# Splitting q and k of fused attention in fewer, wider pieces: block-diagonal last rows, one low part on VectorE, and another order of the period

## The chip, the cores and the metric

The kernel runs on one core of a Trainium2 chip. Times are microseconds of device time for one execution. The core has TensorE (PE in the rows; its weight loads are PEld), VectorE (DVE), ScalarE (ACT), GpSimd (POOL), SyncE (SP, which starts most of the DMA transfers here), a memory on the chip that all of them read (SBUF), and a smaller one for the results of TensorE (PSUM).

## The reference

Attention with a block-causal mask over 8 batches of 8 heads, then a mixture of experts (16 experts in 4 groups, one expert for each token).

```python
B, H, S, D = q.shape                       # 8, 8, 576, 64
scores = scale * np.matmul(q, k.transpose(0, 1, 3, 2))
mask = block_i >= block_j                  # blocks of 64 positions
scores = np.where(mask, scores, -1000000000.0)
scores = scores - np.max(scores, axis=-1, keepdims=True)
attn = np.exp(scores)
attn = attn / (np.sum(attn, axis=-1, keepdims=True) + 1e-09)
attn_out = np.matmul(attn, v)
x = attn_out.transpose(0, 2, 1, 3).reshape(B * S, H * D)   # 4608 x 512
...
g_idx = np.argmax(x @ w_group, axis=1)     # then an expert of the group
h = np.maximum(xg[mask_e] @ w1[g, e], 0.0)
out[tok_idx] = combined[:, None] * (h @ w2[g, e])
```

## The kernel before, in words

The attention works on items. An item is two heads of one batch (the two heads lie in the two halves of the 128 partitions), so there are 32 items, four to a batch. The kernel writes out one period for each item. A period is a list of tokens, `ORDER`, and a token is a letter, a number and a lag: `S3@0` in period x is step S3 of item x, `k1@-1` is step k1 of item x+1. The list is the program order on every engine, and each engine works through its own instructions in that order. A letter `d` behind the lag puts a copying step on VectorE, other copying steps are ScalarE's.

The steps of an item, in the order of its data:

- K: q and k are transposed on TensorE (16 transposes of 64 rows), their first 512 rows. k0 and k1 copy the result to the SBUF tile `nf` (k0 for k, k1 for q times 0.125).
- The last 64 rows of q and k are transposed in step V of an earlier item (`values`), behind its products, into the same PSUM tile `o`. j0 and j1 copy them to `nf`.
- h0 and h1 (`high`) round k and q to the shorter type fp32r, l0 and l1 (`low`) store what rounding left, `nf - high`. The results are in `qk`. For q the last 64 columns are stored block-diagonally, the first head on partitions 0 to 63 and the second on 64 to 127, with zeros elsewhere, so h1 and l1 take three instructions each: 512 columns, and 64x64 twice.
- S3, S2, S1, S8: scores, each the sum of three products in this order: high q with high k, high q with low k (needs l0), low q with high k (needs l1). S2 also does the pair 0.
- D: the row maximum on VectorE. E: the exponential on ScalarE (E6 and E7 belong to S3, E5, E4, E1 and E0 to S2, E3 and E2 to S1, E8 to S8).
- T: transposes of the result on TensorE, t: its copy to SBUF on ScalarE. V: the products with v, v: the copy of the result to `xT`.
- L, n, Y, M, R, X, G, Z: the router and the normalized output of a batch whose four items are done; in each period some of them run. Z are scatters that GpSimd starts.

PSUM gives four buffers of one width in turn (`wide`): every K, S, T, V, L, Y, X and G4 takes the next one, and waits until the tile four places back has been read by all who read it.

The experts follow the attention, on TensorE nearly without a gap. `Attention.start` does the first item ahead of the periods.

Of the kernel before, what the change touches and what calls it, by code (L numbers as in the profile page):

```python
# [48 lines left out]


ORDER, ON_DVE = parse("""
D8@1 Z2@8 E3@1 E2@1 X1@6 K@-1 S3@0 E8@1 k1@-1a S2@0 L0@3 k0@-1a D3@0 E7@0 E6@0 G4@6 D0@0 D2@0 E5@0 G3@6 E0@0
E1@0 R0@3 V@2 T4@1 E4@0 G2@5 G0@4 j0@-1d Z4@9 n0@3a j1@-1d t4@1a v@2d h0@-1 X2@4 T2@1 h1@-1 Y0@3 X0@5 l1@-1
M0@3 T1@1 t2@1a L1@2 T3@0 l0@-1 t0@1a Y1@3 t1@1a t3@0a G1@4 n1@2d S1@0 D1@0 Z0@7 Z1@8 Z3@11 M1@3 S8@0
""")

LAST = [("G", 0), ("G", 1), ("G", 2), ("G", 4), ("G", 3)] + [("X", j) for j in range(3)] + [("Z", j) for j in range(NT)]
# [2 lines left out]
class Attention:  # L60
    def __init__(self, tc, ctx, inner, q, k, v, consts):
        self.tc, self.nc = tc, tc.nc
        self.q, self.k, self.v = q, k, v
        self.c = consts
        self.xpool = ctx.enter_context(tc.tile_pool(name="xp", bufs=2))
        self.pt = ctx.enter_context(tc.tile_pool(name="pt", bufs=2))
        self.small = ctx.enter_context(tc.tile_pool(name="small", bufs=3))
        self.vfix = vfix = ctx.enter_context(tc.tile_pool(name="vfix", bufs=1))
        self.ctx = ctx
        self.psx = ExitStack()  # L70
        self.ps2 = self.psx.enter_context(tc.tile_pool(name="ps2", bufs=4, space=PSUM))
# [100 lines left out]
    def regions(self, i, n):
        al, lo, hi = slice(0, P), slice(0, 64), slice(64, P)
        if n == 0:
            return [(al, slice(0, S), 0)]
        return [(al, slice(0, 512), S), (lo, slice(512, S), S), (hi, slice(512, S), S + BLK)]
# [101 lines left out]
    def values(self, i, N):  # L278
# [1015 lines left out]
```

## Time and profile before

| | |
|---|---|
| median of 3 runs | 861.62 us (860.65 to 863.86) |
| the profiled execution | 854.16 us, of which the span of instructions is 852.4 us |
| PE busy | 796.1 us, 93% of the span |
| VectorE, ScalarE, GpSimd busy | 59%, 58%, 38% |
| mean granted TensorE clock | 0.983 |

The shares are averages over the attention (up to about 371 us), a passage to the experts, and the experts (from about 399 us); the engines are loaded quite differently in them. Rows below give a start and a length in us from the start of the span. Where a group of instructions is printed in one line, "x4" is their count and the shape is that of the first.

### The profile page before, as it was taken

The numbers are of one execution on the slowest core, as the hardware profiler recorded it, in microseconds if no ns is written. First come the engines' busy times: TensorE is split into PE (matmuls) and PEld (weight loads), VectorE is DVE, ScalarE is ACT, GpSimd is POOL, SyncE is SP. The second block draws the span as 40 slices with busy tenths as digits, with TensorE's granted clock in tenths as the row PEclk, the third lists the DMA queues.
The fourth block names the chain that finished last, engine by engine and source line by source line (L and its number), as shares of the span: only waits on it lengthen the run. The fifth ranks groups of instructions, "written<-read, shape, count | busy, mean of one in ns | idle before, by whom it ended". The sixth has DMA issues, their size and how long they took to land.

```text
span 852.4 us, 20362 instructions
## 1 busy us (share of the span) xinstructions
PE 796.1 (93%) x7617; PEld 648.4 (76%) x7617; DVE 500.6 (59%) x1136; ACT 496.0 (58%) x1210; POOL 324.9 (38%) x601
## 2 busy tenths in 40 slices
PE   7789899999999999888999999999999999999996
PEld 4666666666666666566888888888888889898885
DVE  4445868687777676678543454464453755656552
ACT  5877888888888888654332443433443544545441
POOL 5764546474747475643321221221221221132101
PEclk9999999999999999899999999999999999999998
DMA  6554554545454535263443746645555666575471
GB/s 126 137 143 121 152 135 93 135 93 135 93 135 86 142 82 132 62 210 107 155 141 100 237 160 197 202 130 184 196 165 152 189 210 196 180 224 181 150 238 39
DMA packets 182260, 126.69 MB, mean 149 GB/s; under 512 B 124902, under 2 KB 156214, under 8 KB 182160
## 3 DMA queue, kind: packets, MB, share of 16 engines
q1 hardware_dynamic: 173072, 100.73, 42.5%
q0 software_dynamic: 9088, 24.64, 8.5%
q8 instruction: 61, 1.00, 0.5%
q14 instruction: 39, 0.32, 0.1%
HBM read 100.88 MB, written 24.59 MB: 147 GB/s over the span
## 4 chain that ended last, share of the span: by engine, by line
PE 52%; DVE 1%; POOLq 0%; issue 0%; ACT 0%; ACTq 0%
PE y L999 19%; PE h L954 18%; PE y L1004 5%; PE h L949 4%; PE ye L999 2%; PE xp L922 2%; PE he L954 2%; POOLq L1290 0%; DVE gsc L709 0%; DVE gdd L707 0%; DVE goh L711 0%; DVE pre L739 0%; PE spill L609 0%; ACT ys L1021 0%; DVE sel L721 0%
## 5 line engine op out<-in xcount | busy, mean ns | idle before, releaser
L239 ACT ACTIVATE pb<-s,nm 128x512 f32<-128x512 f32 (+4 forms) x288 | 155.6, 556 | 57.0 <-DVE nm L227 51.5
L227 DVE TENSOR_REDUCE nm<-s 128x2 f32<-128x1024 f32 (+4 forms) x160 | 123.3, 807 | 67.2 <-PE s L222 60.9
L954 PE MATMUL h<-xt,wh 128*128 128x264 f32 (+6 forms) x704 | 155.3, 312 | 0.0
L906 DVE TENSOR_TENSOR wl<-raw,wh 128x512 fp32r<-128x512 f32 x192 | 123.3, 685 | 11.2 <-ACT wh L905 10.7
L218 PE MATMUL s<-qk 64*128 64x512 f32 (+3 forms) x768 | 96.0, 361 | 32.6 <-POOL qk L189 18.1
L954 PEld LDWEIGHTS h<-xt,wh 128*128 128x128 f32 x704 | 119.3, 188 | 9.1
L1028 POOL DMA_INDIRECT out_dram<-ys,ids x40 | 41.2, 1030 | 184.7 <-DVE ys L1024 171.2
L905 ACT CAST wh<-raw 128x512 fp32r<-128x512 f32 x192 | 108.8, 620 | 2.2 <-DMA raw<-in_moe_w_dram 1.9
L954 PE MATMUL h<-xt,wl 128*128 128x264 f32 (+6 forms) x352 | 109.3, 311 | 0.0
L999 PE MATMUL y<-wh,hring 128*128 128x512 f32 x306 | 107.2, 401 | 0.0
L272 ACT COPY pt<-tp 128x1024 f32<-128x1024 f32 (+4 forms) x160 | 100.9, 714 | 7.8 <-PE tp L148 6.4
L189 POOL TENSOR_TENSOR qk<-nf,qk 128x512 fp32r<-128x512 f32 (+1 forms) x124 | 101.6, 830 | 7.4
L301 PE MATMUL o<-pt,vb 128*64 128x320 f32 (+4 forms) x896 | 97.1, 370 | 0.0
L967 ACT ACTIVATE hring<-h 128x288 fp32r<-128x288 f32 (+7 forms) x62 | 28.9, 467 | 113.5 <-PE h L954 55.3
L218 PEld LDWEIGHTS s<-qk 64*128 64x128 f32 x768 | 61.5, 196 | 43.7 <-POOL qk L189 23.9
L182 POOL CAST qk<-nf 128x512 fp32r<-128x512 f32 (+1 forms) x127 | 53.7, 448 | 103.9 <-DVE nf L270 100.2
L971 DVE SCALAR_TENSOR_TENSOR hring<-h,hring 128x32 fp32r<-128x32 f32 (+7 forms) x112 | 35.7, 357 | 97.2 <-ACT hring L967 94.0
L301 PEld LDWEIGHTS o<-pt,vb 128*64 128x64 f32 x896 | 61.1, 141 | 36.2 <-issue 6.4
L869 POOL DMA_INDIRECT xg<-xd,ids x40 | 41.2, 1030 | 102.1 <-DMA ids<-tab 51.7
L148 PE MATMUL tp<-ident,pb 64*128 64x64 f32 x1600 | 63.5, 225 | 6.1 <-ACT pb L239 3.9
L954 PEld LDWEIGHTS h<-xt,wl 128*128 128x128 f32 x352 | 66.2, 188 | 1.2
L999 PEld LDWEIGHTS y<-wh,hring 128*128 128x128 f32 x306 | 57.6, 188 | 11.8
(237 smaller groups left out, 1342.8 us busy)
## 6 DMA issues: line engine op xcount, KB each, us to landing
raw<-in_moe_w_dram SPq DMA_DIRECT2D x96, 512.0 KB
natk<-in_k_dram SPq DMA_DIRECT2D x32, 256.0 KB
natq<-in_q_dram SPq DMA_DIRECT2D x32, 256.0 KB
vb<-in_v_dram SPq DMA_DIRECT2D x64, 128.0 KB
wh<-in_moe_w_dram SPq DMA_DIRECT2D x16, 512.0 KB
xd<-xns SPq DMA_DIRECT2D x14, 512.0 KB
tab<-fill POOLq DMA_DIRECT2D x10, 512.0 KB, 3.1
rawe<-in_moe_w_dram SPq DMA_DIRECT2D x8, 512.0 KB
```

Of the source, the lines that this page charges most:

```text
L148: self.nc.tensor.transpose(out=out[:, z], in_=src[r], identity=self.c["ident"][r, r])
L182: eng.tensor_copy(r["qk"][p, 0, a.start + o:a.stop + o], r["nf"][p, n, a])
L189: eng.tensor_tensor(out=r["qk"][p, 1, o], in0=r["nf"][p, n, a], in1=r["qk"][p, 0, o].bitcast(F32), op=ALU.subtract)
L218: nc.tensor.matmul(st[:, z, :], lhsT=t[p, hq, S + P * u:S + P * u + P], rhs=t[p, hk, 0:w], start=x == 0, stop=False)
L227: self.nc.vector.tensor_reduce(out=o, in_=r["s", u], op=ALU.max, axis=ax, negate=True)
L239: nc.scalar.activation(reg, src, AF.Exp, bias=r["nm"][:, t:t + 1], accum_out=self.sms[b][:, pr, z, u:u + 1])
L272: return self.nc.scalar.copy(dst, src)
L301: nc.tensor.matmul(o[64 * a:64 * a + 64, hf, c0:c0 + BLK * (b1 - t)], lhsT=r["v"][:, a, j, :], rhs=pt[:, PTJ * j + t:PTJ * j + b1, a, :], ...
L905: nc.scalar.copy(h[:, sl], s["raw", u][:, sl])
L906: nc.vector.tensor_tensor(out=l[:, sl], in0=s["raw", u][:, sl], in1=h[:, sl].bitcast(F32), op=ALU.subtract)
L954: nc.tensor.matmul(o, lhsT=ww[:, dc, f], rhs=rr[:, dc, t], start=dc == 0 and x == 0, stop=dc == 3 and x == 2)
L999: nc.tensor.matmul(y[c][0:n], lhsT=hh, rhs=w, start=k == 0 and x == 0, stop=k == 7 and x == 2)
```

## The change

Four edits:

1. The last rows of the second head of q are loaded three columns away, beside columns that were set to zero once (`natk` is now a pair of fixed tiles). The transposes then give the block-diagonal form directly (three of them instead of two). `nf` has room for it, j1 copies 128 columns, and h1 and l1 are one instruction each of 640 columns.
2. l0, the low part of k, is on VectorE, one instruction of 576 columns.
3. The order of the period is another one. In it k1 is on VectorE and j0, j1 and v are on ScalarE (before: k1 on ScalarE, j0, j1 and v on VectorE).
4. With the order, lags change: S8 is done a period later, E2 and E3 at the end of their own period, some router steps earlier or later by a period.

```diff
 ORDER, ON_DVE = parse("""
-D8@1 Z2@8 E3@1 E2@1 X1@6 K@-1 S3@0 E8@1 k1@-1a S2@0 L0@3 k0@-1a D3@0 E7@0 E6@0 G4@6 D0@0 D2@0 E5@0 G3@6 E0@0
...
+K@-1 Z3@10 S8@1 k1@-1d S3@0 D8@1 D3@0 k0@-1a S2@0 Z1@9 E8@1 Z4@8 G4@6 E6@0 Z0@8 Z2@9 D0@0 L1@3 E7@0 D2@0
...
-        self.nf = [pfix.tile([P, 2, S], F32, name=f"nf{i}") for i in range(2)]
+        self.nf = [pfix.tile([P, 2 * S + BLK], F32, name=f"nf{i}") for i in range(2)]
+        self.natk = [pfix.tile([P, 12, D], F32, name=f"natk{i}") for i in range(2)]
...
-        for t in self.qk:
-            nc.gpsimd.memset(t.bitcast(F32)[:, :, S + 512:], 0.0)
+        for t in self.natk:
+            nc.gpsimd.memset(t[64:128, 9:11, :], 0.0)
...
-            nc.sync.dma_start(out["k"][64 * z:64 * z + 64, 8:10, :],
+            nc.sync.dma_start(out["k"][64 * z:64 * z + 64, 8:10 + 2 * z:1 + 2 * z, :],
                               src[nm][b, h0:h0 + 2, 512:576, :].rearrange("a p d -> p a d"))
...
+    def flip_last(self, i, ps):
+
+        x = self.lds[i]["k"]
+        for z, n in ((0, 0), (1, 0), (1, 1)):
+            r = slice(64 * z, 64 * z + 64)
+            o = 384 * z + 64 * n
+            self.nc.tensor.transpose(out=ps[:, z, o:o + 64], in_=x[r, 8 + 2 * n:10 + 2 * n, :].rearrange("p a d -> p (a d)"),
+                                     identity=self.c["ident"][r, r])
...
     def full_last(self, i, n):
         r = self.rs[i]
-        self.evac(("j", n), r["nf"][:, n, 512:S], self.last(r["jps"])[:, n], 0.125 if n else None)
...
+        w = 64 + 64 * n
+        self.evac(("j", n), r["nf"][:, S * n + 512:S * n + 512 + w], r["jps"][:, n, 384 * n:384 * n + w], 0.125 if n else None)
+
+    def side(self, tok):
+        return self.nc.vector if tok in self.on_dve else self.nc.gpsimd
 
     def high(self, i, n, eng=None):
         r = self.rs[i]
-        eng = eng or self.nc.gpsimd
-        for p, a, o in self.regions(i, n):
-            eng.tensor_copy(r["qk"][p, 0, a.start + o:a.stop + o], r["nf"][p, n, a])
+        o = slice(S, 2 * S + BLK) if n else slice(0, S)
+        (eng or self.side(("h", n))).tensor_copy(r["qk"][:, 0, o], r["nf"][:, o])
 
     def low(self, i, n, eng=None):
         r = self.rs[i]
-        eng = eng or self.nc.gpsimd
-        for p, a, o in self.regions(i, n):
-            o = slice(a.start + o, a.stop + o)
-            eng.tensor_tensor(out=r["qk"][p, 1, o], in0=r["nf"][p, n, a], in1=r["qk"][p, 0, o].bitcast(F32),
-                              op=ALU.subtract)
+        o = slice(S, 2 * S + BLK) if n else slice(0, S)
+        (eng or self.side(("l", n))).tensor_tensor(out=r["qk"][:, 1, o], in0=r["nf"][:, o], in1=r["qk"][:, 0, o].bitcast(F32),
+                                              op=ALU.subtract)
```

How the order moves the instructions, at three places. First GpSimd, the split of one item. Before (CAST is `high`, TENSOR_TENSOR is `low`; k has 576 columns, q 512 and two squares):

```order
L182 CAST qk_113<-nf_115 128x576
L182 CAST qk_113<-nf_115 128x512
L182 CAST qk_113<-nf_115 64x64 x2
L189 TENSOR_TENSOR qk_113<-nf_115,qk_113 128x512
L189 TENSOR_TENSOR qk_113<-nf_115,qk_113 64x64 x2
L189 TENSOR_TENSOR qk_113<-nf_115,qk_113 128x576
```

and with the change, in a period in which a batch's scale factors (`ry`) are copied too:

```order
L187 CAST qk_113<-nf_115 128x576
L648 COPY ry_4585<-rx_4579 128x2x5x2 x2
L187 CAST qk_113<-nf_115 128x640
L192 TENSOR_TENSOR qk_113<-nf_115,qk_113 128x640
L187 CAST qk_114<-nf_116 128x576
```

Eight instructions of an item became three, and the one for the low part of k is gone from here.

Second VectorE, at the turn from one period to the next, in a period with the router's choice of experts (`esc` to `eoh`). Before:

```order
L707 TENSOR_TENSOR edd_3426<-el_3423,emx_3425 128x20
L709 SCALAR_TENSOR_TENSOR esc_3427<-edd_3426,desc 128x20
L710 TENSOR_REDUCE em_3428<-esc_3427 128x5
L711 TENSOR_TENSOR eoh_3429<-esc_3427,em_3428 128x20
L227 TENSOR_REDUCE nm_3270<-s_1_3437 128x2
L227 TENSOR_REDUCE nm_3270<-s_8_3449 128x1
L227 TENSOR_REDUCE nm_3487<-s_3_3488 128x2
```

and with the change:

```order
L710 TENSOR_TENSOR edd_2487<-el_2484,emx_2486 128x20
L712 SCALAR_TENSOR_TENSOR esc_2488<-edd_2487,desc 128x20
L713 TENSOR_REDUCE em_2489<-esc_2488 128x5
L714 TENSOR_TENSOR eoh_2490<-esc_2488,em_2489 128x20
L192 TENSOR_TENSOR qk_113<-nf_115,qk_113 128x576
L230 TENSOR_REDUCE nm_2333<-s_1_2499 128x2
L273 TENSOR_SCALAR nf_116<-tp_2519 128x512
L230 TENSOR_REDUCE nm_2333<-s_8_2536 128x1
L230 TENSOR_REDUCE nm_2546<-s_3_2547 128x2
```

The low part of k (l0, line 192) and the copy of q (k1, line 273) now stand between the router's steps and the row maxima D1, D8 and D3.

Third ScalarE, from the exponentials of S2 (E4 and its neighbours) to the copies of the transposes. Before:

```order
L239 ACTIVATE pb_117,sm_3485<-s_2_3925,nm_3913 128x384
L272 COPY lt<-lg_0_3942 128x2x288
L272 COPY pt_3844<-tp_4_3987 128x2x5x64
L272 COPY pt_3844<-tp_2_4005 128x2x3x128
L272 COPY pt_3844<-tp_2_4005 128x256
L272 COPY pt_3844<-tp_1_4051 128x2x2x128
L272 COPY pt_4061<-tp_3_4062 128x2x4x128
```

and with the change:

```order
L242 ACTIVATE pb_119,sm_1691<-s_2_1706,nm_1693 128x384
L275 COPY nf_116<-o_1741 128x64
L276 ACTIVATE nf_116<-o_1741 128x128
L275 COPY xT_1324<-o_1741 128x576
L275 COPY pt_1577<-tp_1_1781 128x2x2x128
L275 COPY pt_1577<-tp_4_1790 128x2x5x64
L275 COPY pt_1825<-tp_3_1826 128x2x4x128
L275 COPY pt_1577<-tp_2_1845 128x2x3x128
L275 COPY pt_1577<-tp_2_1845 128x256
```

j0, j1 and v (lines 275 and 276, from `o`) stand behind the last exponential of S2, and the copies t come in another order, with t2 and t0 last.

## Rows read from the trace of the kernel before

**Rows 1.** The time by stage: busy time of each engine in stretches of the span (start:end, length, then us busy and number of instructions for PE, weight loads, VectorE, ScalarE, GpSimd; then the granted TensorE clock, the DMA share and GB/s).

```profile
29.05:101.34 72.29, 61.44 (x869) 45.72 (x865) 38.22 (x78) 55.31 (x154) 42.58 (x98) 0.93 0.52 138
101.34:342.50 241.16, 220.67 (x3495) 166.94 (x3491) 178.46 (x419) 205.34 (x567) 140.03 (x253) 1.00 0.48 114
...
399.00:852.40 453.40, 446.32 (x2490) 386.83 (x2489) 229.92 (x501) 185.35 (x363) 97.46 (x161) 0.99 0.54 170
```

**Rows 2.** Waits, the window from 101.34 to 342.5 us (engine and line, what released it: us in total, times, longest).

```profile
PE s L218 <- POOL mark L782: 10.1, 11, 1.2
PE s L218 <- POOL qk L189: 7.3, 11, 0.7
```

**Rows 3.** TensorE in order of time: starts of the products with v (line 301), one for each period, and two of the waits of line 218 (start us, length us, engine, line, operation, count, idle time before and its releaser).

```profile
29.05 2.93 PE L301 MATMUL o<-pt,vb 128*64 128x256 f32 x28
...
39.21 1.22 PE L218 MATMUL s<-qk 64*128 64x512 f32 x4 [2.66 <-POOL qk L189]
...
42.42 4.37 PE L301 MATMUL o<-pt,vb 128*64 128x256 f32 x28
...
101.34 2.93 PE L301 MATMUL o<-pt,vb 128*64 128x256 f32 x28
...
342.50 2.92 PE L301 MATMUL o<-pt,vb 128*64 128x256 f32 x28
...
354.13 1.22 PE L218 MATMUL s<-qk 64*128 64x512 f32 x4 [4.12 <-POOL mark L782]
...
357.33 2.95 PE L301 MATMUL o<-pt,vb 128*64 128x256 f32 x16
...
364.61 2.92 PE L301 MATMUL o<-pt,vb 128*64 128x256 f32 x28
```

**Rows 4.** One period in order of time, all engines, 199.89 to 214.66 us.

```profile
199.89 2.92 PE L301 MATMUL o<-pt,vb 128*64 128x256 f32 x28
...
202.75 0.27 PE L148 MATMUL o<-ident,natk 64*128 64x64 f32 x2
...
203.51 1.69 POOL L182 CAST qk<-nf 128x576 fp32r<-128x576 f32 x4 [5.64 <-DVE nf L270]
...
205.28 3.43 POOL L189 TENSOR_TENSOR qk<-nf,qk 128x512 fp32r<-128x512 f32 x4
...
208.77 0.73 PE L218 MATMUL s<-qk 64*128 64x512 f32 x4 [0.70 <-POOL qk L189]
...
209.66 2.42 DVE L227 TENSOR_REDUCE nm<-s 128x2 f32<-128x1024 f32 x3 [1.73 <-PE s L222]
...
210.53 0.72 PE L670 MATMUL lg<-xT,wcat 64*32 64x288 f32 x16
...
210.92 0.69 ACT L239 ACTIVATE pb<-s,nm 128x512 f32<-128x512 f32 x1 [1.16 <-DVE nm L227]
...
211.18 2.93 PE L301 MATMUL o<-pt,vb 128*64 128x256 f32 x28
...
214.06 0.67 ACT L272 COPY lt<-lg 128x576 f32<-128x576 f32 x1
...
214.66 3.08 ACT L272 COPY pt<-tp 128x640 f32<-128x640 f32 x5
```

**Rows 5.** Busy time of the engines in the four periods of one batch, 145.03 to 188.76 us (columns as in rows 1).

```profile
145.03:188.76 43.73, 40.02 (x636) 30.32 (x632) 32.51 (x77) 37.28 (x104) 25.84 (x48) 1.00 0.46 111
```

**Rows 6.** Groups of instructions by line and shape, up to 390 us (line, engine, operation, names, shapes, count; us busy, mean ns of one; idle time before).

```profile
L189 POOL TENSOR_TENSOR qk<-nf,qk 128x576 fp32r<-128x576 f32 x31 | 43.5, 1404 | 2.4
L189 POOL TENSOR_TENSOR qk<-nf,qk 128x512 fp32r<-128x512 f32 x31 | 39.8, 1284 | 2.6
...
L189 POOL TENSOR_TENSOR qk<-nf,qk 64x64 fp32r<-64x64 f32 x62 | 19.6, 315 | 2.3
...
L182 POOL CAST qk<-nf 128x576 fp32r<-128x576 f32 x31 | 20.6, 665 | 94.6 <-DVE nf L270 94.5
...
L227 DVE TENSOR_REDUCE nm<-s 128x1 f32<-128x576 f32 x32 | 24.1, 754 | 6.3 <-PE s L208 6.3
...
L270 DVE TENSOR_SCALAR nf<-tp 128x512 f32<-128x512 f32 x1 | 0.7, 692 | 5.8 <-ACT nf L272 5.8
...
L189 DVE TENSOR_TENSOR qk<-nf,qk 128x512 fp32r<-128x512 f32 x1 | 0.7, 717 | 0.0
...
L272 ACT COPY nf<-o-3_167 128x64 f32<-128x64 f32 x1 | 0.2, 217 | 0.0
```

**Rows 7.** VectorE and GpSimd at the same time: a row of each at about 8 us, and three rows of both at about 139 us (start us, length us).

```profile
7.78 0.90 POOL L182 CAST qk<-nf 128x512 fp32r<-128x512 f32 x1 [5.68 <-DVE nf L270]
...
8.24 1.04 DVE L189 TENSOR_TENSOR qk<-nf,qk 128x576 fp32r<-128x576 f32 x1
...
136.02 0.18 DVE L707 TENSOR_TENSOR gdd<-lgs,gmx 128x20 f32<-128x20 f32 x1
...
139.79 3.42 POOL L189 TENSOR_TENSOR qk<-nf,qk 128x512 fp32r<-128x512 f32 x4
...
139.88 1.22 DVE L707 TENSOR_TENSOR edd<-el,emx 128x20 f32<-128x20 f32 x1
```

**Rows 8.** The period that begins at 342.50 us on GpSimd, and a stretch of 2 us with the granted clock (PEclk, 0.50) (columns as in rows 1).

```profile
350.35 0.23 POOL L182 CAST qk<-nf 64x64 fp32r<-64x64 f32 x1 [1.67 <-DMA tab<-pay,pi]
...
42.00:44.00 2.00, 2.00 (x16) 1.54 (x18) 1.29 (x2) 1.42 (x5) 1.13 (x8) 0.50 0.26 68
```

More of the change, by code (lines that the diff above doesn't have):

```diff
@@ L51 @@
 ORDER, ON_DVE = parse("""
-D8@1 Z2@8 E3@1 E2@1 X1@6 K@-1 S3@0 E8@1 k1@-1a S2@0 L0@3 k0@-1a D3@0 E7@0 E6@0 G4@6 D0@0 D2@0 E5@0 G3@6 E0@0
-E1@0 R0@3 V@2 T4@1 E4@0 G2@5 G0@4 j0@-1d Z4@9 n0@3a j1@-1d t4@1a v@2d h0@-1 X2@4 T2@1 h1@-1 Y0@3 X0@5 l1@-1
-M0@3 T1@1 t2@1a L1@2 T3@0 l0@-1 t0@1a Y1@3 t1@1a t3@0a G1@4 n1@2d S1@0 D1@0 Z0@7 Z1@8 Z3@11 M1@3 S8@0
+K@-1 Z3@10 S8@1 k1@-1d S3@0 D8@1 D3@0 k0@-1a S2@0 Z1@9 E8@1 Z4@8 G4@6 E6@0 Z0@8 Z2@9 D0@0 L1@3 E7@0 D2@0
+Y1@4 X2@5 G3@6 E0@0 V@2 n1@3d E5@0 E1@0 E4@0 M1@4 j0@-1a h0@-1a G2@5 j1@-1a Y0@3 T1@1 T4@1 R0@2 X1@5 h1@-1a
+l1@-1a v@2a X0@6 L0@2 t1@1a T3@0 t4@1a n0@2a t3@0a M0@3 T2@1 t2@1a t0@1a G0@4 G1@4 l0@-1d S1@0 D1@0 E2@0
+E3@0
 """)
@@ L124, in load @@
         out, src = {}, dict(k=self.k, q=self.q)
-        for nm, n in (("k", 10), ("q", 8)):
-            out[nm] = self.nat.tile([P, n, D], F32, tag="nat" + nm, name=f"nat{nm}{i}")
+        out["k"], out["q"] = self.natk[i % 2], self.nat.tile([P, 8, D], F32, tag="natq", name=f"natq{i}")
+        for nm in "kq":
             nc.sync.dma_start(out[nm][:, 0:8, :].rearrange("p (c a) d -> p c a d", a=2),
@@ L158, in prep @@
                 self.flip(o[:, :, c, :], ld[nm][:, 2 * c:2 * c + 2, :].rearrange("p a d -> p (a d)"))
-    def last(self, ps):
-        return ps.rearrange("p z (h c) -> p (z h) c", c=64)[:, 0:15:14, :]
+    def flip_last(self, i, ps):
[5 more added lines that the diff above has]
+                                     identity=self.c["ident"][r, r])
@@ L163, in full @@
     def full(self, i, n):
         r = self.rs[i]
-        self.evac(("k", n), r["nf"][:, n, 0:512].rearrange("p (z c) -> p z c", z=2), r["kps"][:, :, 256 * n:256 * n + 256],
-                  0.125 if n else None)
+        self.evac(("k", n), r["nf"][:, S * n:S * n + 512].rearrange("p (z c) -> p z c", z=2),
+                  r["kps"][:, :, 256 * n:256 * n + 256], 0.125 if n else None)
     def full_last(self, i, n):
         r = self.rs[i]
-        self.evac(("j", n), r["nf"][:, n, 512:S], self.last(r["jps"])[:, n], 0.125 if n else None)
@@ L172, in regions @@
[L172 to L176, printed above, removed]
+        w = 64 + 64 * n
+        self.evac(("j", n), r["nf"][:, S * n + 512:S * n + 512 + w], r["jps"][:, n, 384 * n:384 * n + w], 0.125 if n else None)
+    def side(self, tok):
+        return self.nc.vector if tok in self.on_dve else self.nc.gpsimd
@@ L285, in values @@
         if i + 3 < N:
-            self.flip(self.last(o), self.lds[i + 3]["k"][:, 8:10, :].rearrange("p a d -> p (a d)"))
+            self.flip_last(i + 3, o)
     def products(self, i, o):
```

## The prediction

> **What bounds the kernel now.** I read the time by stage first. From 399 us on, TensorE is busy for 446.3 of 453.4 us [rows 1], and the change touches nothing there: this part moves earlier or later as a whole. In the attention TensorE is not full. Over the 22 periods from 101.34 to 342.5 us it is busy 220.7 of 241.2 us at full clock, and in the six from 29.05 to 101.34 us 61.4 of 72.3 us at a granted clock of 0.93 [rows 1]. The waits come next: in the 22 periods TensorE waited 10.1 + 7.3 = 17.4 us for GpSimd, 22 times, once in each period, always at line 218, the scores S3 [rows 2]. The rows of one period show the loop behind it. The products start at 199.89, the last rows are transposed at 202.75, VectorE copies them (j0, j1) until 203.51, GpSimd then rounds (1.69) and subtracts (3.43) until 208.71, the second product of S3 starts at 208.77, and S3, S2 and a router step later the next products start, at 211.18 [rows 4]. Of these 11.3 us GpSimd holds 5.2. All four periods of a batch take 43.73 us, 10.93 each [rows 5].
>
> So the question is what loop is longest once GpSimd's part shrinks. I price three of them.
>
> **TensorE.** It is busy 40.02 us in a batch [rows 5]; one more small transpose in each period adds about 0.04. Floor: 10.05 a period.
>
> **ScalarE.** It gains v (0.60, the distance from the 576-wide copy at 214.06 to the next start at 214.66 [rows 4]), j0 and j1 (0.33 together, an estimate from 0.217 for 64 columns [rows 6] less overlap), and loses k1 (about 0.5). From 37.28 a batch [rows 5] it comes to about 39. Its loop: S3 waits, by the ring of four PSUM buffers, until t0, the last of the copies t, has drained the tile of T2. From the start of S3 to E6 it is 0.29 for its first pair of products (four take 0.57), 0.89 (208.77 to 209.66) and 1.26 (to 210.92) = 2.44; E6 to the end of S2's exponentials is 3.14 (210.92 to 214.06), the five copies 3.08 [rows 4]. With j0, j1, v and 0.08 for the hand-over: 2.44 + 3.14 + 0.93 + 3.08 + 0.08 = 9.67.
>
> **GpSimd and VectorE.** GpSimd's parts: h0 0.65 and h1 about 0.69 (0.665 for 576 columns [rows 6]), l1 at 640 columns 1.52 (1.284 at 512 and 1.404 at 576, so 0.12 more; bounds: 1.40, and 1.72 for 576 and a 64x64 piece [rows 6]). l0 on VectorE: 0.717 at 512 columns [rows 6], 0.78 at 576. Taken alone that is off the path. But the trace shows that the two engines hold each other up. `edd` on VectorE, two inputs from SBUF, takes 0.18 like its twin `gdd` at 136.02 when it is alone; at 139.88 it took 1.22 and ended at 141.10, when GpSimd's 512-wide subtraction, begun at 139.79, had run its 1.28. At 7.78 GpSimd's cast took 0.90 beside VectorE's work, and VectorE's 576-wide subtraction 1.04 instead of 0.78 right after it [rows 7]. l0 has two SBUF inputs, and it follows h0, so it falls just where h1 and l1 run. If VectorE comes to it while l1 runs, it is held to l1's end.
>
> The Trainium skill, SBUF — State Buffer, section "SBUF: two separate sides", has a rule for this: a VectorE instruction with two SBUF inputs and a GpSimd instruction that reads SBUF take turns, the later one blocked for the whole of the other. The trace agrees (1.22 instead of 0.18). By that rule the sum below is the one with the hold, 835; without it, it would be 827.
>
> When does VectorE come to l0? In every period of a batch it does router work before it, 2 to 5 us of it after D0 (D0 ends 1.16 after E6: 209.66 + 2.42 [rows 4]). l1 runs from E6 + 4.73 to E6 + 6.25: 3.14 to j0, 0.23 for it, 0.65, 0.69 and 0.02, then 1.52. VectorE arrives at about + 5.5 to + 7, within or after l1. So l0 ends 0.62 after l1, at + 6.87, and behind it stand D1, k1, D8 and D3 (the order shows it). With 0.08 of overlap for each: D1 at + 6.80, k1 0.61 later, D8 0.61 later (0.692 less overlap [rows 6]), D3 0.67 later (0.754 [rows 6]), and the next E6 1.26 after that: 9.95. This loop and ScalarE's are near each other, and the router's part of each period comes on top:
> - Period with L1 and Y0: L1 (0.65, 210.53 to 211.18 [rows 4]) delays V, so j0 comes 0.44 later: 10.4.
> - Period with Y1: the choice of experts is twelve dependent small instructions, 0.2 apart, some with two SBUF inputs. They run beside h0, h1 and l1 and are held by them; `esc` comes after l1, and l0 begins about + 7.0 and ends + 7.8: 10.9.
> - Period with X2 and X1: GpSimd's index step 0.15 and V 0.06 later: 10.2.
> - Period with G4, X0 and L0: two small GpSimd copies 0.34 give 10.3; TensorE has some 1.4 us of router work, and S8 ends late for S3: 10.5.
>
> Sum 42.0 a batch, 10.5 a period.
>
> **The sum,** against the profiled execution (854.16 us, 852.4 of span):
> - 22 periods: 241.2 / 43.73 = 5.5 batches x 1.73 = -9.5.
> - The six first periods: 72.3 us, 12.05 each [rows 1, 3]. GpSimd also does set-up there; TensorE waited 2.66 for it at 39.21, after which its clock was granted 0.50 (1.2 GHz) and the products at 42.42 took 4.37 instead of 2.92 [rows 3, 8]. There is little router work, so VectorE reaches l0 while h1 runs, goes in before l1, and l1 ends later, still ahead of S3's third product. 9.95, with some set-up between h0 and l1 10.3: 61.8. -10.5.
> - The period from 342.50 to 357.33 (14.83 [rows 3]): five scatters stood between the two halves of the split, one small cast waited 1.67 for them [rows 8], and S3 waited 4.12 [rows 3]. Now four scatters run while GpSimd is idle and one lies between h0 and h1: 10.6. -4.2. The next one (7.28) began at the lower clock (the four products at 354.13 took 1.22 where they take 0.73 [rows 3, 4]): -0.7.
> - The two periods before 29.05: the same loops without V, t and v: -1.0.
> - The passage to the experts: v of the last item leaves VectorE, where it stands ahead of a step that TensorE waits for: -0.5.
>
> The loads on SP's queue are the same in number and size and come a whole period ahead; l0's removal, the zeroing in `natk` and the wider j1 (0.1) are hidden by the loops above. Total -26.4: 854.2 becomes 828. The runs' median is 861.62, 7.5 above the profiled execution; I keep that distance: **835**.
>
> **The rivals.**
> - *The hold costs little* (VectorE gets in before l1, or arrives after it). For it: turns are short around 139 us, `esc` was not held. Then TensorE and ScalarE bound: 10.25, 9.9, 10.0 and 10.5 with the same router terms, 40.6 a batch, -17.2 instead of -9.5: **827**.
> - *The hold costs in all periods what it costs with Y1* (10.9): the steady part stays as before, only the first periods, the stalled one and the ends gain, -16.9: **845**.
> - *Slower: l1 costs much more at 640 columns.* GpSimd's 64x64 piece takes 0.315 for 64 columns, 4.9 ns each [rows 6]; at that price l1 is 3.15, 1.6 more in each period. 22 periods then take 267 instead of 241 (+26), the first six gain 1.5, the stalled one about 2.6, the rest 1.5: about +20, **882**. It decides from l1 = 2.5 us on (26.4 over 28 periods is 0.94 more). Against it: 512 to 576 columns cost 1.9 ns each [rows 6].
> - *The gains cancel*: ScalarE's 39 of 42 us leaves no slack, each late hand-over costs, and the steady periods lose what the first gain: about 860.
>
> **How the numbers follow.** Forecast 0.46 (its own range 829 to 842), hold costs little 0.22, hold everywhere 0.17, slower 0.08, cancelled 0.07. Holding 8 in 10 leaves out the slow case and half of the cancelled one: 825 to 853. About 0.5% (4.3 us) is what a measurement of this kernel tells from no change: faster 0.85, same 0.06, slower 0.09.
>
> **What would show it.** Each step right: TensorE's wait for GpSimd at S3 gone or under 0.3 us; GpSimd three instructions an item, l1 about 1.5 us; l0 on VectorE lengthened well beyond 0.78 in the 22 periods and ending with or after l1; ScalarE waiting for D1 or D3; batches of about 42 us; clock 1.00 between 29 and 101 us. Wrong: l0 at 0.7 to 0.8 and batches near 40.6 (first rival); waits of TensorE for ScalarE's copies t, v at S3, T2 or S1 (the ring) with periods over 11; l1 over 2 us; the experts no longer moving as a block.

## The result, and the profile after

The changed kernel takes 836.55 us (median of 4 runs, 836.34 to 836.70) against 861.14 us of the kernel before on the same chip: a ratio of 0.9708, 95% interval 0.9687 to 0.9729. Its profiled execution took 836.7 us, with 835.0 of span.

The time by stage in the changed kernel (columns as in [rows 1]; the last row is one batch, as [rows 5]).

```profile
0.00:32.80 32.80, 26.22 (x255) 17.47 (x255) 16.57 (x25) 18.34 (x53) 11.90 (x28) 0.84 0.60 131
32.80:93.84 61.04, 58.10 (x874) 43.88 (x870) 42.31 (x73) 56.23 (x166) 32.19 (x68) 1.00 0.60 165
93.84:325.13 231.29, 219.96 (x3516) 168.28 (x3512) 201.76 (x399) 211.39 (x611) 100.38 (x151) 1.00 0.51 116
325.13:353.51 28.38, 23.07 (x352) 17.80 (x344) 18.73 (x59) 20.33 (x58) 11.94 (x17) 1.00 0.44 133
...
146.19:188.21 42.02, 39.85 (x638) 30.51 (x635) 36.62 (x73) 38.35 (x112) 18.12 (x27) 1.00 0.49 114
```

The reader is to see three things. The six first periods took 61.04 us at a granted clock of 1.00 (72.29 at 0.93 before, [rows 1]). A batch took 42.02 (43.73, [rows 5]), with GpSimd at 18.12 us in place of 25.84 and VectorE at 36.62 in place of 32.51. And the stretch up to the first products with v is longer, 32.80 us (29.05, [rows 3]).

In the waits of the changed kernel from 93.84 to 325.13 us (engine, line, releaser: total, times, longest) no row of TensorE names GpSimd any more; [rows 2] had 17.4 us there. What TensorE waits for now is ScalarE, at S2 (the waits of the last row, for which the profile shows no releaser, stand at S2 too). ScalarE in turn waits for row maxima of VectorE, the first row:

```profile
ACT pb L242 <- DVE nm L230: 13.8, 38, 0.9
...
PE s L221 <- ACT pb L242: 5.6, 11, 0.9
...
PE s L221 <- issue: 4.0, 5, 0.9
```

The two groups of GpSimd's l1 and VectorE's l0 (up to 390 us, columns as in [rows 6]):

```profile
L192 POOL TENSOR_TENSOR qk<-nf,qk 128x640 fp32r<-128x640 f32 x31 | 49.8, 1606 | 2.6
...
L192 DVE TENSOR_TENSOR qk<-nf,qk 128x576 fp32r<-128x576 f32 x32 | 42.6, 1330 | 16.5 <-POOL qk L187 16.4
```

l0 takes 1.33 us on the mean; the shortest, 0.745, is what it needs alone. One period shows why (changed kernel, start and length):

```profile
150.59 0.72 POOL L187 CAST qk<-nf 128x640 fp32r<-128x640 f32 x1
...
151.39 1.56 POOL L192 TENSOR_TENSOR qk<-nf,qk 128x640 fp32r<-128x640 f32 x1
...
151.62 1.95 DVE L192 TENSOR_TENSOR qk<-nf,qk 128x576 fp32r<-128x576 f32 x1
153.49 0.68 DVE L230 TENSOR_REDUCE nm<-s 128x2 f32<-128x512 f32 x1
...
154.20 0.47 ACT L242 ACTIVATE pb<-s,nm 128x256 f32<-128x256 f32 x1 [0.33 <-DVE nm L230]
```

l1 ends at 152.95, l0 at 153.57, 0.62 later; then comes D1, for which ScalarE waits 0.33 us. Behind D1 VectorE goes on without a gap through k1, D8 and D3, and the next item's E6 starts at 156.60:

```profile
153.49 0.68 DVE L230 TENSOR_REDUCE nm<-s 128x2 f32<-128x512 f32 x1
154.09 0.68 DVE L273 TENSOR_SCALAR nf<-tp 128x512 f32<-128x512 f32 x1
154.69 3.16 DVE L230 TENSOR_REDUCE nm<-s 128x1 f32<-128x576 f32 x4
```

In two of the batch's other periods l0 also ends 0.62 after l1. In the fourth, the one with the choice of experts, `esc` is held in its place, and l0 comes after l1 and takes 0.75:

```profile
172.17 1.54 POOL L192 TENSOR_TENSOR qk<-nf,qk 128x640 fp32r<-128x640 f32 x1
172.24 1.51 DVE L712 SCALAR_TENSOR_TENSOR esc<-edd,desc 128x20 f32<-128x20 f32 x1
```

The stages of every profile, worked out from the starts of the products with v (us; "22" are five and a half batches; "29th" is the period that began at 342.50 before; "batch" is one batch where it is steady):

| kernel | first V | six | 22 | 29th | 30th | 31st | rest | batch |
|---|---|---|---|---|---|---|---|---|
| before | 29.05 | 72.29 | 241.16 | 14.83 | 7.28 | 6.81 | 481.0 | 43.73 |
| before, 2nd profile | 30.10 | 72.69 | 246.91 | 14.90 | 6.97 | 6.81 | 481.2 | 44.90 |
| changed | 32.80 | 61.04 | 231.29 | 11.82 | 7.02 | 9.54 | 481.5 | 42.02 |
| changed, 2nd profile | 29.32 | 60.99 | 231.22 | 9.85 | 6.98 | 9.27 | 479.6 | 42.02 |
| no l1 | 28.71 | 58.64 | 218.82 | 9.12 | 6.82 | 11.49 | 479.9 | 39.70 |
| wide only | 31.52 | 64.24 | 230.93 | 13.45 | 7.96 | 6.80 | 478.7 | 41.72 |
| order only | 35.29 | 78.07 | 244.20 | 12.48 | 7.96 | 6.47 | 478.3 | 44.07 |
| l0 first on GpSimd | 33.61 | 65.17 | 228.27 | 11.19 | 7.96 | 9.11 | 482.4 | 41.54 |
| l0 with one input | 31.65 | 60.82 | 224.68 | 10.39 | 6.81 | 7.99 | 481.8 | 40.83 |
| both low on VectorE | 31.61 | 60.94 | 226.13 | 11.06 | 6.82 | 10.32 | 478.2 | 41.10 |
| D1 ahead of l1 | 31.44 | 59.72 | 248.40 | 12.19 | 7.76 | 6.47 | 481.5 | 44.41 |
| both, and the sum | 31.51 | 60.94 | 226.05 | 11.06 | 6.82 | 6.48 | 480.5 | 41.09 |
| changed, and the sum | 32.81 | 61.05 | 231.24 | 9.85 | 6.98 | 6.47 | 482.4 | 42.02 |
| the same, in experiment 5 | 29.21 | 60.97 | 231.19 | 9.85 | 6.98 | 6.47 | 481.0 | 42.01 |

### The profile page after: what moved, and what is told of

It reads as the page before. It is cut to its first block, busy times and chain, and to the rows that moved or that the text cites. A ratio compares the mean times of both kernels' runs of the same rounds, so it can differ in the third digit from the quotient of the medians.

```text
span 835.0 us, 20289 instructions
## 1 busy us (share of the span) xinstructions
PE 795.5 (95%) x7649; PEld 649.7 (78%) x7649; DVE 529.3 (63%) x1102; ACT 504.6 (60%) x1273; POOL 265.9 (32%) x444
## 4 chain that ended last, share of the span: by engine, by line
PE 54%; DVE 1%; issue 0%; POOLq 0%; ACT 0%; ACTq 0%
PE y L1002 20%; PE h L957 19%; PE y L1007 5%; PE h L952 4%; PE ye L1002 2%; PE xp L925 2%; PE he L957 2%; POOLq L1293 0%; DVE gsc L712 0%; DVE gdd L710 0%; DVE goh L714 0%; DVE pre L742 0%; PE spill L612 0%; ACT ys L1024 0%; DVE sel L724 0%
## 5 line engine op out<-in xcount | busy, mean ns | idle before, releaser
L909 DVE TENSOR_TENSOR wl<-raw,wh 128x512 fp32r<-128x512 f32 x192 | 123.4, 685 | 11.2 <-ACT wh L908 10.6
L230 DVE TENSOR_REDUCE nm<-s 128x2 f32<-128x1024 f32 (+4 forms) x160 | 122.9, 801 | 11.1 <-PE s L225 5.8
L221 PE MATMUL s<-qk 64*128 64x512 f32 (+3 forms) x768 | 90.8, 351 | 12.6 <-ACT pb L242 7.3
L1031 POOL DMA_INDIRECT out_dram<-ys,ids x40 | 41.2, 1029 | 183.4 <-DVE ys L1027 170.0
L304 PE MATMUL o<-pt,vb 128*64 128x320 f32 (+4 forms) x896 | 93.9, 360 | 1.1 <-issue 1.1
L187 POOL CAST qk<-nf 128x640 fp32r<-128x640 f32 (+1 forms) x63 | 43.0, 694 | 150.8 <-ACT nf L275 140.4
L221 PEld LDWEIGHTS s<-qk 64*128 64x128 f32 x768 | 58.9, 190 | 24.8 <-issue 11.2
L150 PE MATMUL tp<-ident,pb 64*128 64x64 f32 x1600 | 65.5, 227 | 7.6 <-ACT pb L242 6.8
L150 PEld LDWEIGHTS tp<-ident,pb 64*128 64x128 f32 x1600 | 58.1, 141 | 14.3 <-ACT pb L242 8.0
```

The costliest lines, as they stand in the source:

```text
L150: self.nc.tensor.transpose(out=out[:, z], in_=src[r], identity=self.c["ident"][r, r])
L187: (eng or self.side(("h", n))).tensor_copy(r["qk"][:, 0, o], r["nf"][:, o])
L221: nc.tensor.matmul(st[:, z, :], lhsT=t[p, hq, S + P * u:S + P * u + P], rhs=t[p, hk, 0:w], start=x == 0, stop=False)
L230: self.nc.vector.tensor_reduce(out=o, in_=r["s", u], op=ALU.max, axis=ax, negate=True)
L304: nc.tensor.matmul(o[64 * a:64 * a + 64, hf, c0:c0 + BLK * (b1 - t)], lhsT=r["v"][:, a, j, :], rhs=pt[:, PTJ * j + t:PTJ * j + b1, a, :], ...
L909: nc.vector.tensor_tensor(out=l[:, sl], in0=s["raw", u][:, sl], in1=h[:, sl].bitcast(F32), op=ALU.subtract)
```

## The experiments

Under "Measured" stand the ratio to the kernel before, timed beside it on the same chip, with its 95% interval, and the median time.

**1. l1 left out.**

```diff
+        for t in self.qk:
+            nc.gpsimd.memset(t.bitcast(F32)[:, 1, S:], 0.0)
...
     def low(self, i, n, eng=None):
+        if n == 1:
+            return
```

> The changed kernel with l1 left out: GpSimd does h0 and h1 only, and the low part of q is zeroed once at the start (so the products with it add nothing). All instructions of VectorE, ScalarE and TensorE stay where they are. Theory (VectorE's l0 is held until GpSimd's l1 ends, and D1, k1, D8, D3 stand behind it): with l1 gone the hold falls, l0 takes close to 0.78 us in nearly all periods, the batch of four periods goes from 42.0 to about 40.6 us, and the time from 836.5 to about 828. Rival A (ScalarE's loop of 9.67 us and the router's parts alone set 42.0; the hold is hidden): l0 gets short, the batch stays at 41.8 to 42.0, the time at 835 to 837. Rival B (h0 and h1 hold it as much): l0 stays near 1.3 us and the batch near 42.0.

Measured: 0.9528 (0.9505 to 0.9551), 815.64 us. The batch, and then the group of l0 from 100 to 300 us:

```profile
136.68:176.38 39.70, 39.39 (x638) 30.54 (x635) 33.06 (x73) 37.91 (x111) 11.56 (x23) 1.00 0.54 122
```

```profile
L196 DVE TENSOR_TENSOR qk<-nf,qk 128x576 fp32r<-128x576 f32 x20 | 15.0, 748 | 0.0
```

l0 is never held now, and the batch falls by 2.3 us, more than the 1.4 that I expected: TensorE is busy 39.39 of 39.70 us and is the bound. ScalarE's work (37.91) does not set 42.0: rival A is out. h0 and h1, which stayed, do not hold l0 (0.748 on the mean): rival B is out too.

**2. l0 with one input.** It asks whether l1's hold on VectorE, not l1's own end, sets the period.

```diff
     def low(self, i, n, eng=None):
...
+        if n == 0 and eng is None:
+            self.nc.vector.tensor_scalar(out=r["qk"][:, 1, o], in0=r["nf"][:, o], scalar1=0.0, scalar2=None, op0=ALU.mult)
+            return
```

> The changed kernel with l0 on VectorE replaced by an instruction of the same 576 columns with one SBUF input (nf times zero; the low part of k is thus zero). GpSimd's h0, h1 and l1 are unchanged. Theory (an instruction with two SBUF inputs is what GpSimd's work holds): it takes about 0.45 us, as the rounding of the same size did at the start, and is not lengthened beside l1; the next row maximum starts 0.5 to 1 us earlier after l1's begin; batches of 39.8 to 40.5 us. Rival A (any VectorE instruction that reads and writes SBUF is held): 0.8 to 1.4 us, batches of 41.5 to 42. Rival B (l1's end bounds the period by S3's third product, not by VectorE): short instruction, batches of 41.5 to 42 and TensorE waits for GpSimd.

Measured: 825.87 us in one run. GpSimd's l1 and VectorE's instruction in one period, the same instruction in another, and then the batch:

```profile
148.42 1.56 POOL L195 TENSOR_TENSOR qk<-nf,qk 128x640 fp32r<-128x640 f32 x1
...
148.65 1.65 DVE L193 TENSOR_SCALAR qk<-nf 128x576 fp32r<-128x576 f32 x1
...
170.53 0.45 DVE L193 TENSOR_SCALAR qk<-nf 128x576 fp32r<-128x576 f32 x1
```

```profile
143.22:184.05 40.83, 39.48 (x639) 30.51 (x636) 35.45 (x73) 38.33 (x112) 17.71 (x27) 1.00 0.51 119
```

My theory was wrong in one point: the instruction with one input is held too, 1.65 us instead of 0.45. But it ends 0.32 after l1's end (150.30 and 149.98) where l0 ended 0.62 after it. These 0.30 us, four times, are the 1.2 us by which the batch is shorter (42.02 to 40.83): each of its four periods is shorter by 0.3, also the one in which the instruction comes after l1 and takes 0.45 instead of 0.75. So it is rival A's hold, and yet a shorter batch: the end of VectorE's instruction is paid in full. TensorE does not wait for l1, so rival B is out; its waits from 92.47 to 317.15 us are these alone:

```profile
PE s L224 <- ACT pb L245: 5.3, 13, 0.8
PE s L214 <- ACT pt L278: 1.0, 5, 0.2
```

The Trainium skill, SBUF — State Buffer, section "SBUF: two separate sides", names a second kind of VectorE instruction that takes turns with GpSimd beside the one with two SBUF inputs: those in a two-port mode. The 0.45 us for 576 columns where two inputs take 0.75, and the hold, agree with it.

**3. The parts of the change apart.** The wide pieces alone, in the old order and on the old engines; the new row of the period alone, with the narrow pieces; and l0 taken back to GpSimd, behind h0:

```diff
-ORDER (changed)
+ORDER (before)                          # wide only
-ORDER (before)
+ORDER (changed)                         # order only, in the kernel before
- ... j0@-1a h0@-1a G2@5 ... l0@-1d S1@0 ...
+ ... j0@-1a h0@-1a l0@-1a G2@5 ... S1@0 ...   # l0 first on GpSimd
```

> The wide pieces alone: block-diagonal load, one h1 and one l1, but order and engines of the kernel before (l0 last on GpSimd, j0, j1 and v on VectorE, k1 on ScalarE). Theory: GpSimd's 5.2 us an item become 0.65 + 0.72 + 1.56 + 1.40 = 4.33, which is 0.87 less, and TensorE's wait of 0.79 a period for GpSimd at S3 goes to nearly nothing; batches of about 40.6 us, six first periods about 66, time about 842 (838 to 846). Rival (the old order's next loop is close behind: copies of ScalarE, or VectorE's j0 and j1 behind the row maxima): batches of 42.5 to 43.5 us, time 852 to 858, and the order is what brings most.

> The new order alone: pieces as in the kernel before (q's last rows split in 64x64 pieces, six instructions an item on GpSimd, l0 on GpSimd, since that kernel knows no other engine for it), the row of the period and the engines of j0, j1, v, k1 from the changed kernel. Theory: GpSimd needs 5.2 us from j1 on, so l0 ends 0.9 us later than it would with wide pieces and TensorE waits for it at S3; the batch is 42.5 to 44 us, the time 845 to 861. Rival (the order alone brings the gain, GpSimd's length is covered since S3 stands further back): batches of 42.0 us or less and a time of 836 to 840.

> The changed kernel with l0 on GpSimd directly behind h0 (order h0, l0, h1, l1). VectorE loses l0 and its hold; GpSimd has 0.65 + 1.40 + 0.72 + 1.56 = 4.33 us an item, from E6 + 3.4 to E6 + 7.7, when the third product of S3 needs l1 at about E6 + 7.8. Theory of the hold: batches of 40.6 to 41.2 us, time 828 to 832. Rival A (ScalarE's loop sets 42.0): no change, 835 to 837. Rival B (S3 waits for l1, as it waited for l0 before the change): TensorE waits over 0.5 us a period for GpSimd at S3, batches of 42.5 to 43.5 us, time 840 to 848.

Measured: wide only 0.9793 (0.9758 to 0.9829), 836.66 us; order only 1.0135 (1.0114 to 1.0156), 867.27 us; l0 first 0.9797 (0.9777 to 0.9818), 838.81 us. A batch of the first and of the third, and the waits of order only from 113.36 to 357.56 us:

```profile
147.49:189.21 41.72, 39.54 (x638) 30.47 (x636) 33.58 (x77) 37.18 (x103) 23.10 (x31) 1.00 0.51 117
```

```profile
150.21:191.75 41.54, 40.01 (x638) 30.32 (x636) 32.95 (x69) 37.83 (x111) 23.24 (x31) 1.00 0.50 116
```

```profile
PE s L219 <- POOL qk L190: 14.9, 16, 1.1
...
PE s L219 <- POOL mark L783: 5.7, 6, 1.0
```

The wide pieces alone take 2.1% off, the whole change 2.7% on the same chip (experiment 4). Their batch (41.72) lies between the 40.6 that I expected and the rival's 42.5, their time a little under the 838 to 846 that I gave. In the 22 periods they bring all of the gain: 230.93 us against 231.2, although one of their periods took 11.65 where its like took 10.15. The new order with l0 on VectorE gains outside, by the table against the second profile of the changed kernel: 3.3 us in the six first periods (64.24 to 60.99), where GpSimd also has set-up to do, 3.6 in the 29th (13.45 to 9.85) and 1.0 in the 30th; it loses 2.5 in the 31st. The new order without the wide pieces is slower than no change: TensorE waits 14.9 + 5.7 = 20.6 us for GpSimd, more than the 17.4 of before. That is the mechanism I expected, and it cost more: the batch took 44.07, and the time is over the 845 to 861 that I gave. And l0 on GpSimd is no worse than l0 held on VectorE in the steady batch (41.54), but costs 4.2 us in the six first periods. Of my expectations for "l0 first" none fits: the hold is gone, TensorE does not wait for GpSimd in the 22 periods, and the batch is 41.5, not 40.6 to 41.2; what bounds it there I did not take apart.

**4. The changed kernel again,** with no edit.

> The changed kernel once more, beside the others of this group and with a second profile. If the time of this kernel is steady and it was the kernel before that ran slow in its first timing (861 against a profiled execution of 854): 835 to 837 again, so a ratio of 0.971 to 0.977 depending on the kernel before. If the gain by the order and by l0's new engine over the wide pieces alone is real (0.971 against 0.979): about 832 where the kernel before takes 857. For the ramp: if its 3.75 us were the clock of that one execution, the first products with v start at 29 to 31 us in this profile; if they come from the new row (j0 and j1 behind exponentials on ScalarE, l0 held), they start at 32.5 to 33.5 us again.

Measured: 0.9730 (0.9704 to 0.9757), 831.59 us (828.95 to 833.63) against 855.6. Both kernels ran about 5 us faster here than where the result was taken. The eight filling products of the start, in order of time, in the first profile of the changed kernel and then in the second; behind them the stretch from 24 to 28 us of each (granted clock third from the end):

```profile
6.47 3.60 PE L313 MATMUL wps<-pb 128*128 128x512 bf16 x8
```

```profile
6.31 1.90 PE L313 MATMUL wps<-pb 128*128 128x512 bf16 x8
```

```profile
24.00:28.00 4.00, 2.70 (x46) 2.55 (x42) 1.24 (x1) 4.00 (x12) 2.44 (x3) 0.51 0.38 86
```

```profile
24.00:28.00 4.00, 3.92 (x68) 3.36 (x68) 3.09 (x4) 4.00 (x12) 3.78 (x4) 1.00 0.27 62
```

The same instructions take two courses from one execution to the next. The first V at 32.8 goes with 3.60 us for those products (also in "changed, and the sum"), the one at 29.3 with 1.90 (also in experiment 5, at 29.21). So most of the longer ramp in the first profile is not the new row. The eight products alone do not set the first V, though: "both low on VectorE" and "both, and the sum" have the same start, 1.90 and 3.21 us for these products, and the first V at 31.61 and 31.51. The 29th period has two courses as well, 11.82 in the first profile and 9.85 in the three others of this row. In the first profile TensorE stopped in the middle of its products for no wait that the profile shows, and D0 and D2 on VectorE, whose scores S2 end at 324.56 in the records, began at 327.21:

```profile
327.16 1.76 PE L304 MATMUL o<-pt,vb 128*64 128x320 f32 x16 [0.62 <-issue]
```

```profile
327.21 1.29 DVE L230 TENSOR_REDUCE nm<-s 128x2 f32<-128x256 f32 x2 [2.61 <-remote]
```

In the second profile the same row maxima (at 321.00) waited for nothing.

**5. The sum lgs of the last batch but one on VectorE.**

```diff
-                nc.gpsimd.tensor_tensor(out=st["lg"], ...
+                (nc.vector if b == 6 else nc.gpsimd).tensor_tensor(out=st["lg"], ...
```

> The changed kernel with one small addition moved: the sum lgs of the last batch but one goes from GpSimd, where it waited behind four gathers, to VectorE, right behind the reduction that it needs. Theory (the chain of choices of experts waited 5.58 us for it on VectorE, with D1 and D8 of the last item behind): the period from 343.97 to 353.51 goes from 9.54 to 6.8 to 7.3 us, the time down by 2 to 2.7. Rival (the new order of that chain ahead of D1 costs, or the passage waits for something else): that period stays at 9 us or over.

Measured: 827.43 us in one run. In the changed kernel the sum stood behind the gathers on GpSimd, and VectorE's chain of choices behind it; then the same two instructions with the edit, and its last products:

```profile
343.15 1.00 POOL L872 DMA_INDIRECT xge<-xd,idse  x1 [0.27 <-POOL xge L871]
344.18 0.40 POOL L697 TENSOR_TENSOR lgs<-lps 128x100 f32<-128x100 f32 x1
...
344.61 0.18 DVE L709 TENSOR_REDUCE gmx<-lgs 128x5 f32<-128x20 f32 x1 [5.58 <-POOL lgs L697]
```

```profile
333.32 0.26 DVE L697 TENSOR_TENSOR lgs<-lps 128x100 f32<-128x100 f32 x1
333.62 0.17 DVE L709 TENSOR_REDUCE gmx<-lgs 128x5 f32<-128x20 f32 x1
...
344.67 2.92 PE L304 MATMUL o<-pt,vb 128*64 128x256 f32 x28
```

The period is 6.47 us instead of 9.27: the cause is shown. Of the 2.8 us, 1.4 are given back later (the rest is 481.0 instead of 479.6): in the first expert's products TensorE's granted clock was 0.83 from 352.3 to 362.2, where it was 1.00 at the same place of the changed kernel's second profile.

**6. Both subtractions on VectorE,** as a test of the hold and as a candidate; with l1 one place later, behind D1, and the sum of experiment 5; and each of the two orders that held their ground with that sum.

```diff
- ... h1@-1a l1@-1a v@2a ... l0@-1d S1@0 D1@0 E2@0
+ ... h1@-1a v@2a ... l0@-1d l1@-1d S1@0 D1@0 E2@0     # both
+ ... h1@-1a v@2a ... l0@-1d S1@0 D1@0 l1@-1d E2@0     # D1 ahead of l1
```

> The changed kernel with l1 moved too: both subtractions on VectorE, l0 and then l1 right behind it, GpSimd keeps h0 and h1 alone. Theory (what costs is GpSimd's 1.56 us for l1 and the hold on VectorE while it runs): l1 takes about 0.86 on VectorE, from l0's 0.75 and 0.1 for 64 more columns; l0 goes in beside h1, l1 ends near E6 + 6.3 instead of l0's E6 + 6.87, so about 0.5 a period less: batches of 39.8 to 40.4 us, six first periods about 59, time about 822 to 826. Rival A (VectorE, busy 36.6 of 42 us, becomes the bound, since it gains 0.86 an item): VectorE busy 36.5 to 37 us a batch, ScalarE waits for it, batches of 41 to 42 us, 832 to 838. Rival B (h0 and h1 on GpSimd hold the two as long as l1 did): l0 and l1 near 1.4 each, batches of 42 to 43, 836 to 845.

> Both subtractions on VectorE as in the run before with l1 there, but l1 one place later, behind D1 (l0, D1, l1, k1, D8, D3), and the sum lgs of the last batch but one on VectorE. Theory: with l0 and l1 ahead of D1 the exponentials E2 and E3 came 0.82 us later than need be; now D1 stands where it stood without l1 and l1 still ends ahead of S3's third product, so batches of 40.0 to 40.6 us in place of 41.1, the last period 6.5 to 7 in place of 10.3: 22 periods at 221.5, time 819 to 823, the fastest of the kernels that compute everything. Rival A (S3 waits for l1): TensorE waits 0.3 to 0.8 us a period for VectorE at S3, batches of 41 to 42. Rival B (what bounds 41.1 is the place of k1, D8 and D3, all of which still stand behind l1): batches of 40.8 to 41.1, time 823 to 825.

> Both subtractions on VectorE, l0 and l1 together ahead of D1 (the order whose batches took 41.1 us), and the sum lgs of the last batch but one on VectorE. The two gains lie in different stretches, so they should add: 22 periods 226 to 227 us, the last period 6.5 to 7 us instead of 10.3, a ratio to the kernel before of 0.963 to 0.967. If the wait that cost the run with D1 ahead of l1 its gain comes from this kernel's timing too (row maxima that start over 0.5 us after VectorE came free, at the same place in each batch): batches of over 42 us and a ratio over 0.970.

> The changed kernel with the sum lgs of the last batch but one on VectorE, timed this time, beside the other of this group. Its last period was 6.47 us instead of 9.27: a ratio to the kernel before of 0.969 to 0.971, 2 to 3 us under the changed kernel's 0.971 to 0.973, and 3 to 5 us over the other of this group.

Measured: both 0.9684 (0.9658 to 0.9709), 827.72 us; D1 ahead of l1 0.982 (0.9799 to 0.984), 844.65 us; both and the sum 0.9659 (0.9641 to 0.9678), 825.24 us; changed and the sum 0.9711 (0.9687 to 0.9735), 832.23 us. The batch of "both" and its two groups from 100 to 300 us:

```profile
143.65:184.75 41.10, 39.52 (x638) 30.57 (x635) 35.67 (x77) 38.25 (x112) 11.97 (x23) 1.00 0.51 117
```

```profile
L192 DVE TENSOR_TENSOR qk<-nf,qk 128x640 fp32r<-128x640 f32 x19 | 15.6, 818 | 0.0
L192 DVE TENSOR_TENSOR qk<-nf,qk 128x576 fp32r<-128x576 f32 x19 | 14.3, 750 | 0.0
```

l0 and l1 take 0.75 and 0.82 and are not held, yet the batch is 41.10, not the 39.8 to 40.4 of the theory. Both now stand ahead of D1, 0.82 us more than without l1; D1 begins 0.3 to 1.6 us after the end of S1, with no gap on VectorE before it. That this is what costs is argued and not shown: moving D1 ahead was to mend it and did the opposite. In "D1 ahead of l1", the end of S1 (its mask products), D1, and S3's third product:

```profile
161.82 0.20 PE L225 MATMUL s<-mk,mq 64*128 64x64 bf16 x2
...
164.28 0.69 DVE L230 TENSOR_REDUCE nm<-s 128x2 f32<-128x512 f32 x1 [1.51 <-PE s L211]
...
165.76 0.50 PE L221 MATMUL s<-qk 64*128 64x512 f32 x2 [1.25 <-DVE qk L192]
```

S1 ends at 162.02 in the records, D1 starts 2.26 us later, and l1, now behind it, keeps TensorE waiting 1.25 us. It comes in the same period of each of the five batches from 100 to 300 us, and one later period takes 16.84. The wait for l1 is rival A's, but it is a part only: 7.9 us in the 22 periods, which took 248.40 where "both" took 226.13. Why D1 is so late stays open, and so does what 41.10 could fall to. This order ran on chip 11 alone, where the kernel before has late row maxima too (experiment 7), so the runs do not separate the order from the chip.

"Both and the sum" is the fastest kernel that computes everything: 0.8% under the changed one with the same sum, beside it on the same chip. Its 22 periods (226.05), its last one (6.48) and its ratio are as I expected; its distance to the changed kernel with the sum is 7.0 us, not 3 to 5. The sum alone cannot be told from the changed kernel in time (0.9711 and 0.973), with the 2.8 us of its period lying within the 3.5 us of the two courses of the ramp.

**7. The kernel before again,** with no edit.

> The kernel before once more, for a second profile of it on the chip of the other experiments. If the 6 to 7 us by which its timed runs lay above its profiled execution (861 against 854) are a matter of the chip: about 855 here, with the same 43.7 us a batch, and 5 to 6 us less than the first timing in any kernel. If they are executions that differ within (the stalled period of 14.83 us, the low clock of the first six periods): the first six periods differ from 72.3 us, or the stalled one from 14.83, by over 2 us.

Measured: 861.32 us in one run. It fell on another chip (chip 11) than the other experiments (chip 7, but for "D1 ahead of l1"); its other runs there took 858.0 to 863.5. The end of S2, D2 and D0, and the batch:

```profile
146.42 0.20 PE L222 MATMUL s<-mk,mq 64*128 64x64 bf16 x2
```

```profile
147.91 1.29 DVE L227 TENSOR_REDUCE nm<-s 128x2 f32<-128x256 f32 x2 [1.00 <-PE s L222]
```

```profile
146.55:191.45 44.90, 40.08 (x636) 30.24 (x632) 32.52 (x77) 37.60 (x104) 25.91 (x48) 1.00 0.44 107
```

Of the 7.2 us between its two profiles' spans (852.4 and 859.6), 5.75 lie in the 22 periods: in five of the six batches one period is about 12.1 instead of 11.1, as row maxima start 1.0 to 1.3 us after the records' end of their scores, where in the first profile VectorE went on without a gap. Neither case of the expectation is met: the first named a chip on which this run was not, and the six first periods (72.69) and the stalled one (14.90) differ by far less than the 2 us of the second. But the times of this kernel go by chip: all its 21 runs on chip 7 took 854.0 to 857.1 us, and all 14 others, on chip 11 and where the result was taken, 858.0 to 863.9. The profiled 854.16 fits chip 7 alone; where it was taken is not on record. The late row maxima go the same way: in the ten profiles from chip 7 and in this kernel's first, VectorE never stood idle over 0.6 us behind the end of the scores that a row maximum reads; on chip 11 it did nine times here and ten times in "D1 ahead of l1", and in the changed kernel's first profile once. This supports the first case. Why these row maxima are late, no run here shows.

## Why the prediction was right, and where it was not

The forecast of 835 (825 to 853, faster) is met by 836.55. By its steps, from the first profile of the kernel before to the first and the second of the changed kernel (the second is the one to compare, as the last point says):

| step | forecast | first | second |
|---|---|---|---|
| 22 periods | -9.5 | -9.9 | -9.9 |
| six first periods | -10.5 | -11.2 | -11.3 |
| period at 342.50 | -4.2 | -3.0 | -5.0 |
| the next one | -0.7 | -0.3 | -0.3 |
| the last period | 0 | +2.7 | +2.5 |
| ramp | -1.0 | +3.7 | +0.3 |
| passage and rest | -0.5 | +0.5 | -1.4 |
| sum | -26.4 | -17.5 | -25.2 |

- **The hold: right, mechanism and size.** l0 ends 0.62 after l1, as forecast (the prediction gives this number without its working), and the batch is 42.0. Experiments 1 and 2 show that this end sets the period. The split over the four periods is good to 0.2 as well: from E6 to E6, as they were priced, they took 10.62, 10.72, 10.23 and 10.45 where I had 10.4, 10.9, 10.2 and 10.5. With the choice of experts the held one was `esc`, which I had placed behind l1.
- **The six first periods: right on the mean** (10.17 for 10.3). In four of them l0 went in before l1, as forecast; three took 9.5 to 9.7 and three 10.7, not one length.
- **l1 at 640 columns: right** (1.56 us, forecast 1.52), so the slower rival had no ground.
- **The rival "hold costs little": wrong size.** Without the hold I gave 40.6; without l1 it is 39.70. Its floor for TensorE, 10.05 a period from [rows 5], was too high: its busy time fell to 39.39 a batch.
- **The ramp, -1.0: wrong.** "The same loops" gained nothing there; and I did not know that its course differs by 3.5 us between executions.
- **The last period: a step left out.** I priced that GpSimd's queue would clear at 342.50, and did not ask what its gathers would hold up two periods on, with the chain of choices now ahead of D1 on VectorE.
- **"I keep that distance", 7.5: a step without a reason, and right in the main.** I did not ask why the timed runs lay above the profile. The kernel before takes 861.14 where the result was taken and 855.6 on chip 7, the changed one 836.55 and 831.59: some 5 us of the distance go with the place, and both kernels have them. So the -17.5 of the first profiles is no measure of the sum: it sets an execution at the lower level against one at the higher. Medians on the same chip fell by 24.6 and 24.0 us: the sum was 2 us too large, the forecast 1.5 us too low.

## What to carry to other kernels

Before moving elementwise work from GpSimd to VectorE, look whether GpSimd still runs a long instruction at that time: here 0.75 us of work became 1.15 to 1.95, and when its end came 0.30 us sooner, each period was 0.30 shorter. Merging narrow pieces brought three quarters of the gain with none of that. One profile is one execution on one chip: compare two of the same kernel, and take both kernels on the same chip, before the difference is given to an edit.

## What the runs showed of the hardware that I had not expected

- A VectorE instruction with one SBUF input, 0.45 us alone, took up to 1.65 us beside GpSimd's subtraction.
- Eight equal products (128x512, bf16) took 1.90 us in nine profiles and 3.00 to 3.60 in five, while the rows give a granted clock of 1.00 for both. The seven like them that come first took 3.06 to 3.17 in every profile, 0.45 each, which is the pace of the 3.60; so a granted clock of 1.00 in a row did not mean the faster pace.
- In three profiles row maxima on VectorE began late (1.3, 2.3 and 2.7 us in the rows above) after the records' end of the scores that they read, with VectorE idle. Two of these profiles are the only ones from chip 11, the third is the changed kernel's first. In the ten from chip 7 none did. No run here shows the cause.
